# A new order for all engines' tasks in a forgetting-attention and gated-convolution kernel

## The chip, the core and the metric

The kernel runs on one core of a Trainium2 chip. A core has five engines that run side by side, each on its own instruction stream: PE (matrix multiply), DVE (vector), ACT (scalar functions), POOL (a slower general engine) and SP, which here does nothing but start DMAs. Each engine takes its instructions strictly in the order in which they were written. The metric is the device time of one execution in microseconds (us).

## The reference

Attention with a forgetting gate over 8 batches of 8 heads, 576 positions and 64 channels, and behind it a feed-forward layer with a convolution over the positions and a gate. Cut to what is computed:

```python
# _attn_ref(q, k, v, f)
scores = scale * np.matmul(q, k.transpose(0, 1, 3, 2))
log_f = np.log(np.clip(f, 0.0001, 1.0))
cum = np.cumsum(log_f, axis=-1)
decay = cum[:, :, :, None] - cum[:, :, None, :]
scores = np.where(causal, -1000000000.0, scores + decay)
attn = np.exp(scores - max); attn = attn / (sum + 1e-09)
return np.matmul(attn, v)
# _moe_ref(x, w_in, conv_w, w_out), x of shape (8, 576, 512)
h = np.maximum(x @ w_in, 0.0)                       # 512 -> 1024
conv_out += conv_w[k][None, None, :] * hp[:, k:k + S, :]   # three taps
gate = 1.0 / (1.0 + np.exp(-conv_out))
return (h * gate @ w_out)                           # 1024 -> 512
```

All inputs and the output are float32.

## The kernel before

The work is cut into tasks. A function `add(name, engines, after, fn, take, give, behind)` declares each: which engine may run it, what has to be done before it, and which buffers it takes and gives back. A table, `ORDER`, lists all the tasks in one row. `Plan.play` walks this row and calls each task's function at once, so the row is the program: every engine's instruction stream is the row with the other engines' tasks left out. Where a task may run on several engines, the row names one behind an `@`. Nothing sorts the tasks afterwards. Buffers are handed out first come, first served as the row is walked, so a task placed behind another may also get that one's buffer and must then wait for its reader.

The names. `hb` is half a batch, four heads, 0 to 15; `i` a pair of heads, two to an `hb`; `b` a batch; `ff` a block of 128 of the 1024 hidden channels.

- Loads on SP: `ld` (q and k of the first two `hb` as they are), `q` (q or k of a later `hb`, by a transposing DMA), `v`, `wi` and `wo` (the two weight matrices in four parts each).
- Decay: `dca` (DVE), `dcl` (ACT, a logarithm), `dcs` and `dck` (DVE) make the running sums; `ki` writes them to an image in DRAM, and `rw` or `fi` (three DMAs per `hb`, two for `rw`) fetch the rows of an `hb` from that image into its q and k tile, so that one matmul gives scores and decay. Of `hb` 0 the decay comes from extra matmuls instead, so it does not need `ki`.
- Setup: `tp` (PE) transposes the plainly loaded q and k, `cl` (DVE or ACT) copies them out or prepares the rows; `cw` (PE) and `cwt` (DVE) lay out the convolution's weights; `wic`, `woc` cast the weights to 16 bits and `va` casts v.
- Attention: `sd`, `so`, `st` (PE) make the diagonal, off-diagonal and last-64 scores; `ed`, `eo`, `et` (ACT) the exponentials; `md`, `mt` (POOL) mask where PE did not; `pv` (PE) multiplies with v in two parts; `n` and `m` (DVE) divide; `t` and `tx` turn the result for the next layer.
- Feed-forward: `f` (PE, first matmul), `r` (ACT, relu), `c` and `d` (DVE, the convolution), `a` (ACT, gate), `g` (DVE, product), `o` (PE, second matmul), `e` (ACT or DVE, out of PSUM), `s` (store).

PE writes into four PSUM tiles (`ps`) that all its tasks share. Five tiles `ht` hold `r`'s results until `g`, four tiles `u` hold `c`'s until `a`, four tiles `ob` stage weights and outputs, and four q and k tiles form a ring over `hb`. SP's and ACT's DMAs draw on eight semaphores in turn.

The lines to know in the profile are 159 (`ld`), 166 (`tp`), 172 and 174 (`cl` on ACT and DVE), 180 (`q`), 186 (`cl` of later rows), 204 and 205 (`rw`), 211 (`v`), 219 and 221 (`va`), 281 (`ki`), 296 (`cw`), 314, 317, 319 and 322 (scores), 355 and 372 (exponentials), 391 and 396 (`pv`), 407 (`m`), 416 and 419 (`t`, `tx`), 431 (`f`), 448 and 450 (`c`, `d`), 476 (`o`), 492 (the last `e`), 518 (`wi`, `wo`), 526 (`wic`, `woc`). The heart of `play`:

```python
for x in order:
    name, _, engine = x.partition("@")
    t = self.tasks[name]
    assert all(a in done for a in t["after"] + t["behind"]), name
    for r in t["take"]:
        self.slot[name, r] = free[r].pop(0)
    ...
    for r, taker in t["give"]:
        free[r].append(self.slot[taker, r])
```

## Time and profile before

| what | value |
|---|---|
| time, three runs | 245.07, 245.49 and 247.19 us, median 245.49 |
| profiled execution | span 244.7 us from its first to its last instruction; no other time of it is kept |
| busy in the span | PE 228.6 us (93%), ACT 206.8 (85%), DVE 205.5 (84%), POOL 51.9 (21%) |
| DMA | 49.68 MB, mean 203 GB/s; SP's queue carries 48.81 MB |

The profile is one execution. The median of the runs lies 0.8 us above its span. A line number stands for a function, so a group of instructions of one line is one kind of task; the number behind x is a count. In the table by windows each stretch has the busy time of every engine, the share of the full TensorE clock that was granted, and the mean load of the DMA engines. "PE ps L391 <- DVE va L219" in the table of waits reads: PE, about to write a `ps` tile at line 391, sat idle until DVE had written `va` at line 219. The chain of waits follows the last instruction back to what released it, step by step.

### The profile page before, as it was taken

To read this page: it belongs to the slowest core of one execution; us is meant where nothing else is said; L and a number is where in the kernel's file an instruction comes from. 1 tells how busy PE (TensorE), PEld (TensorE's weight loads), DVE (VectorE), ACT (ScalarE), POOL (GpSimd) and SP (SyncE) were. 2 spreads that over 40 slices of the span, in tenths; PEclk is the share of its full clock that TensorE was granted. 3 is DMA by queue.
4 is the path that set the end of the run, shared out by engine and by line. 5 is a ranking of instruction groups with operands and counts; after the bars stand their busy time and mean duration, and the time that the engine had idled before them with its cause. 6 is when DMAs were issued, how large, how long until landed. Compare 5 with 4: busy or idle time off the path is not lost.

```text
span 244.7 us, 6393 instructions
## 1 busy us (share of the span) xinstructions
PE 228.6 (93%) x2627; PEld 146.1 (60%) x2627; DVE 205.5 (84%) x324; ACT 206.8 (85%) x278; POOL 51.9 (21%) x77
## 2 busy tenths in 40 slices
...
GB/s 189 334 169 250 278 184 189 223 198 306 196 216 196 169 182 220 238 268 251 224 212 274 194 198 269 270 102 196 265 198 227 195 209 4 106 173 77 171 85 216
DMA packets 120424, 49.68 MB, mean 203 GB/s; under 512 B 109879, under 2 KB 110647, under 8 KB 120395
## 3 DMA queue, kind: packets, MB, share of 16 engines
q1 hardware_dynamic: 120073, 48.81, 89.9%
q10 hardware_dynamic: 322, 0.47, 0.6%
...
HBM read 21.11 MB, written 10.17 MB: 128 GB/s over the span
## 4 chain that ended last, share of the span: by engine, by line
PE 81%; DMA 5%; DVE 5%; ACT 5%; issue 1%; SPq 1%; ACTq 0%; DVEq 0%
PE ps L476 26%; PE ps L431 23%; PE ps L314 15%; PE ps L391 7%; DMA qk<-image 3%; PE ps L322 3%; PE ps L396 3%; DMA u<-in_f_dram 2%; PE ps L416 2%; ACT qk L172 2%; DVE u L450 2%; DVE u L448 1%; ACT ht L442 1%; ACT pp L372 1%; PE ps L317 1%
## 5 line engine op out<-in xcount | busy, mean ns | idle before, releaser
L431 PE MATMUL ps<-xt,w_in_f 128*128 128x512 f16 (+1 forms) x512 | 71.0, 288 | 0.4 <-DVE xt L419 0.4
L372 ACT ACTIVATE pp<-ps 128x1024 f16<-128x1024 f32 x64 | 64.8, 1032 | 3.7 <-PE ps L314 2.3
L476 PE MATMUL ps<-w_out_f,hg 128*128 128x512 f16 x288 | 66.8, 379 | 0.0
L314 PE MATMUL ps<-qk 128*128 128x128 bf16 (+2 forms) x576 | 63.9, 241 | 2.1 <-DMA qk<-image 0.9
L448 DVE SCALAR_TENSOR_TENSOR u<-ht,cwt 128x576 f32<-128x576 f16 x64 | 52.4, 832 | 4.4 <-ACT ht L442 4.2
L450 DVE SCALAR_TENSOR_TENSOR u<-ht,cwt,u 128x576 f32<-128x576 f16 x64 | 53.9, 856 | 0.5
L453 ACT ACTIVATE hg<-u,cw 128x576 f16<-128x576 f32 x64 | 48.7, 782 | 6.1 <-DVE u L450 6.0
L431 PEld LDWEIGHTS <-w_in_f 128*128 128x128 f16 x512 | 34.7, 99 | 29.4 <-issue 1.3
L314 PEld LDWEIGHTS <-qk 128*128 128x128 bf16 x576 | 39.4, 98 | 19.2 <-issue 2.5
L442 ACT ACTIVATE ht<-ps 128x576 f16<-128x576 f32 x64 | 41.0, 664 | 6.4 <-PE ps L431 2.8
L476 PEld LDWEIGHTS <-hg 128*128 128x128 f16 x288 | 26.9, 98 | 28.9
L460 DVE SCALAR_TENSOR_TENSOR hg<-hg,ht 128x576 f16<-128x576 f16 x51 | 38.6, 767 | 0.6 <-ACT hg L453 0.5
L358 POOL TENSOR_SCALAR_AFFINE_SELECT pp<-pd 128x1024 f16<-128x1024 f32 x16 | 19.7, 1244 | 53.6 <-ACT pd L355 53.6
L391 PE MATMUL ps<-va,pp 128*128 128x65 f16 x640 | 25.3, 194 | 1.7 <-DVE va L219 1.7
L391 PEld LDWEIGHTS <-pp 128*128 128x128 f16 x640 | 23.0, 98 | 4.2 <-DVE va L219 1.9
L407 DVE TENSOR_TENSOR xm<-ps,rc 128x896 f16<-128x896 f32 (+1 forms) x32 | 23.9, 751 | 0.5
L355 ACT ACTIVATE pp<-ps 128x1024 f16<-128x1024 f32 x16 | 16.6, 1038 | 5.2 <-PE ps L314 4.0
L219 POOL CAST va<-vf 128x1024 f16<-128x1024 f32 x8 | 10.0, 1247 | 34.3 <-PE ps L314 18.8
L355 ACT ACTIVATE pd<-ps 128x1024 f32<-128x1024 f32 x16 | 16.2, 1023 | 1.2 <-PE ps L314 0.5
L405 DVE RECIPROCAL rc<-ps 128x14 f32<-128x14 f32 (+1 forms) x32 | 6.6, 207 | 10.2 <-PE ps L396 4.9
L322 PE MATMUL ps<-mask,ident 128*128 128x512 bf16 (+1 forms) x40 | 14.4, 364 | 0.4 <-ACT pp L372 0.3
L481 ACT COPY ob<-ps 128x1024 f32<-128x1024 f32 (+1 forms) x14 | 12.9, 918 | 0.3 <-issue 0.2
...
## 6 DMA issues: line engine op xcount, KB each, us to landing
...
```

The lines of the kernel that those rows point to most:

```text
L314: nc.tensor.matmul(o, tk[:, h * S + k0:h * S + k0 + 128], tq[:, h * S + q0:h * S + q0 + n], start=first, stop=last and not by_matmul(hb, h))
L355: nc.scalar.activation(o, ps_of(f"sd{i}").rearrange("p (s c) -> p s c", s=2), AF.Exp, scale=SCALE)
L372: nc.scalar.activation(pair(i)[:, s, 512:1536], ps_of(f"so{i}.{s}"), AF.Exp, scale=SCALE)
L391: nc.tensor.matmul(ps[:, c:c + D + 1], block(hb, h, m, n), va[:, h, m, 0:D + 1], start=(m == 0), stop=(m == n))
L407: nc.vector.tensor_tensor(xm[:, CUT * D * u:CUT * D * u + nj * k * D].rearrange("p (j x d) -> p j x d", x=k, d=D), got[:, :, :, 0:D], r.un ...
L431: nc.tensor.matmul(ps[:, t0:t1], w_in_f16[:, cc, 128 * ff:128 * (ff + 1)], xt[:, cc // 2, x:x + t1 - t0], start=(cc == 0), stop=(cc == NCC ...
L442: nc.scalar.activation(ht_of(b, ff)[:, 2:2 + S], ps_of(f"f{b}.{ff}")[:, 0:S], AF.Relu, scale=1.0 if (b, ff) in LATE else 0.5)
L448: nc.vector.scalar_tensor_tensor(u, ht[:, 1:1 + S], cwt[:, ff, 0:1], ht[:, 2:2 + S], op0=ALU.mult, op1=ALU.add)
L450: nc.vector.scalar_tensor_tensor(u, ht[:, 3:3 + S], cwt[:, ff, 1:2], u, op0=ALU.mult, op1=ALU.add)
L453: nc.scalar.activation(hg_of(b, ff), u_t[slot[f"c{b}.{ff}", "u"]], AF.Sigmoid if (b, ff) in LATE else AF.Tanh, scale=cw[:, ff, 1:2])
L460: nc.vector.scalar_tensor_tensor(hv, hv, 1.0, ht_of(b, ff)[:, 2:2 + S], op0=ALU.add, op1=ALU.mult)
L476: nc.tensor.matmul(ps[:, 512 * j:512 * (j + 1)], w, w_out_f16[:, ff, :], start=(ff == 0), stop=(ff == NFF - 1))
```

## The change

Only the table `ORDER` is different; it now also runs over 52 lines more, so every later line of the new file has a number that is higher by 52 (159 becomes 211, and 211 becomes 263). The set of tasks is the same. 38 tasks change their engine:

- from DVE or ACT to POOL: `va1.1`, `va2.0`, `va3.0`, `va4.0`, `va7.0`, `va7.1`, `va8.0`, `va8.1`, `va9.0`, `va10.1`, `va11.1`, `va12.1`, `va14.0`, `va15.0`; from POOL to DVE or ACT: `va0.0`, `va0.1`, `va1.0`, `va9.1`, `wic0`
- from ACT to DVE: `cl0.0.0`, `va3.1`, `va5.1`, `va15.1`, `tx10`, `e1.1`, `e1.2`, `e2.0`, `e3.2`, `e7.4`; from DVE to ACT: `cl1.0.1`, `tx0`, `tx6`, `tx7`, `tx8`, `e4.0`, `e7.3`
- DMAs from SP to ACT's queue: `ki`, `rw1`, `rw6`, `s7.2`, `s7.0`; from ACT's to SP's: `rw4`, `rw5`

```diff
 ORDER = """
-dca cw ld0 ld1 ld0.0.0 tp0.0.0 dcl ld0.1.0 ld0.0.1 tp0.0.1 tp0.1.0 v0.0 ld0.1.1 ld1.0.1 ld1.0.0 dcs dck ...
+ld0 dca ld0.0.0 ld1 ld0.0.1 ld1.0.0 tp0.0.0 tp0.0.1 cl0.0.0@DVE ld1.0.1 dcl ld0.1.0 ld0.1.1 tp1.0.0 cl0.0.1@ACT v0.0
+tp1.0.1 dcs cl1.0.1@ACT v0.1 tp0.1.0 tp0.1.1 cl0.1.0@ACT v0.3 v0.4 dck q2.0 sd0 cl0.1.1@DVE tp1.1.0 v0.2 cl1.0.0@ACT
...
```

On PE the program no longer begins with `cw`: the first tasks are `tp0.0.0 tp0.0.1 tp1.0.0 tp1.0.1 tp0.1.0 tp0.1.1 sd0`, and `cw` follows seven tasks of scores and transposes later, behind `so0.1`. Up to the first `f0.0`, PE runs the same set of tasks as before, in another sequence; the same is true from `f0.0` to `sd9`.

SP near its start, from the end of the first v loads to the rows of `hb` 2 (`qk_86` and `qk_87` are the q and k tiles of `hb` 1 and 2, `vf_90` is v of batch 1, `ob` holds a part of `w_in`). Before:

```order
L281 DMA image<-kc 64x576 x3
L180 DMA_TRANSPOSE qk_87<-in_k_dram 128x2304
L180 DMA_TRANSPOSE qk_87<-in_q_dram 128x2304
L518 DMA ob_125<-in_moe_w_in_dram 128x2x512
L204 DMA qk_86<-image 1x2304
L205 DMA qk_86<-image 2x2304
L518 DMA ob_126<-in_moe_w_in_dram 128x2x512
L518 DMA ob_127<-in_moe_w_in_dram 128x2x512
L518 DMA ob_128<-in_moe_w_in_dram 128x2x512
L204 DMA qk_87<-image 1x2304
L205 DMA qk_87<-image 2x2304
```

Now, at the same place:

```order
L263 DMA vf_89<-in_v_dram 128x8x64 x3
L263 DMA vf_89<-in_v_dram 64x8x64
L232 DMA_TRANSPOSE qk_87<-in_q_dram 128x2304
L263 DMA vf_89<-in_v_dram 128x8x64
L232 DMA_TRANSPOSE qk_87<-in_k_dram 128x2304
L570 DMA ob_125<-in_moe_w_in_dram 128x2x512
L263 DMA vf_90<-in_v_dram 128x8x64
L570 DMA ob_126<-in_moe_w_in_dram 128x2x512
L256 DMA qk_87<-image 1x2304
L257 DMA qk_87<-image 2x2304
L570 DMA ob_127<-in_moe_w_in_dram 128x2x512
```

`ki` and the rows of `hb` 1 have left SP's queue, the rows of `hb` 2 stand behind two parts of `w_in` instead of four, and the transposing loads no longer stand behind `ki`.

ACT in the same stretch, from its first copy of q and k to its second exponential and a little on (`image<-kc` is `ki`, `pp` are exponentials, `pt` the last-64 ones). Before:

```order
L172 ACTIVATE qk_85<-ps_130,lim 128x1152
L172 ACTIVATE qk_85<-ps_131,lim 128x1152
L172 ACTIVATE qk_85<-ps_132,lim 128x1152
L355 ACTIVATE pp_95<-ps_131 128x2x512
L372 ACTIVATE pp_95<-ps_132 128x1024
L372 ACTIVATE pp_95<-ps_131 128x1024
L172 ACTIVATE qk_86<-ps_129,lim 128x1152
L355 ACTIVATE pp_96<-ps_132 128x2x512
```

Now:

```order
L407 ACTIVATE pp_95<-ps_132 128x2x512
L224 ACTIVATE qk_86<-ps_130,lim 128x1152
L333 DMA image<-kc 64x576 x3
L424 ACTIVATE pp_95<-ps_132 128x1024
L407 ACTIVATE pp_96<-ps_131 128x2x512
L256 DMA qk_86<-image 1x2304
L257 DMA qk_86<-image 2x2304
L386 ACTIVATE pt_101<-ps_129 128x256
L271 CAST va_92<-vf_89 128x4x4x64
L424 ACTIVATE pp_96<-ps_132 128x1024
```

ACT now starts `ki` and the rows of `hb` 1 itself, between its exponentials, and behind them stand `et0`, a cast of v and the rest of `hb` 0's exponentials.

POOL from its first cast on (`va_93` and `va_94` are v of `hb` 2 and 3). Before:

```order
L219 CAST va_91<-vf_89 128x4x4x64
L221 CAST va_91<-vf_89 64x4x64
L526 CAST w_in_f_69<-ob_125 128x2x512
L219 CAST va_92<-vf_89 128x4x4x64
L526 CAST w_in_f_69<-ob_126 128x2x512
```

Now:

```order
L578 CAST w_in_f_69<-ob_125 128x2x512
L273 CAST va_92<-vf_89 64x4x64
L578 CAST w_in_f_69<-ob_126 128x2x512
L578 CAST w_in_f_69<-ob_128 128x2x512
L271 CAST va_93<-vf_90 128x4x4x64
L273 CAST va_93<-vf_90 64x4x64
L271 CAST va_94<-vf_90 128x4x4x64
```

The casts of `hb` 2 and 3 that DVE and ACT had are POOL's now, and one of `w_in`'s four parts has gone to DVE.

More of the change, by code (lines that the diff above doesn't have):

```diff
@@ new lines @@
+ld0 dca ld0.0.0 ld1 ld0.0.1 ld1.0.0 tp0.0.0 tp0.0.1 cl0.0.0@DVE ld1.0.1 dcl ld0.1.0 ld0.1.1 tp1.0.0 cl0.0.1@ACT v0.0
+tp1.0.1 dcs cl1.0.1@ACT v0.1 tp0.1.0 tp0.1.1 cl0.1.0@ACT v0.3 v0.4 dck q2.0 sd0 cl0.1.1@DVE tp1.1.0 v0.2 cl1.0.0@ACT
+ed0 tp1.1.1 sd1 so0.1 cl1.1.1@ACT ki@ACT cl1.1.0@DVE cw cl2.0 q2.1 st0 eo0.1 wi1 ed1 rw1@ACT va0.0@DVE et0 so1.0
+va1.0@ACT eo1.0 so0.0 eo0.0 so1.1 v1.0 sd2 eo1.1 sd3 so3.0 va0.1@DVE cl2.1 ed2 pv0.0 wi2 cwt ed3 rw2@SP n0.0 wic1@POOL
+eo3.0 so2.1 m0.0 so2.0 wi0 pv0.1 n0.1 eo2.1 eo2.0 wic0@DVE so3.1 va1.1@POOL q3.1 m0.1 sd5 q3.0 eo3.1 ed5 pv1.0 st1 et1
@@ new lines @@
+t0 n1.0 pv1.1 m1.0 n1.1 tx0@ACT so5.1 m1.1 t1 tx1@DVE eo5.1 cl3.1 sd4 ed4 f0.0 r0.0 cl3.0 c0.0 so4.1 eo4.1 f0.1 d0.0
+r0.1 wi3 so4.0 q4.1 f0.2 c0.1 eo4.0 d0.1 r0.2 v1.3 wic2@POOL f0.3 rw3@SP h0 v1.2 a0.0 so5.0 r0.3 v1.1 wic3@POOL c0.2
+st2 g0.0 f0.4 v1.4 d0.2 c0.3 eo5.0 et2 sd6 va2.0@POOL sd7 r0.4 c0.4 cl4.1 so7.0 d0.3 so7.1 ed6 d0.4 ed7 eo7.0 so6.1
+pv2.0 f0.5 va2.1@POOL eo7.1 n2.0 q4.0 pv2.1 a0.4 v2.0 q5.0 wo3 m2.0 g0.4 cl4.0 rw4@SP so6.0 eo6.1 r0.5 va3.0@POOL f0.6
+eo6.0 n2.1 st3 c0.5 a0.3 v2.4 va3.1@DVE et3 pv3.0 r0.6 a0.1 pv3.1 d0.5 a0.2 n3.0 q5.1 m2.1 m3.0 wo1 n3.1 t2 g0.2 m3.1
@@ new lines @@
+g0.1 wo2 tx2@ACT f0.7 r0.7 sd9 a0.5 cl5.0 t3 so9.0 sd8 ed9 tx3@DVE wo0 c0.6 c0.7 eo9.0 so9.1 d0.6 f1.0 cl5.1 f1.1
+rw5@SP eo9.1 ed8 f1.2 g0.5 st4 r1.0 a0.6 v2.1 woc3@POOL d0.7 r1.1 f1.3 woc1@POOL g0.3 et4 g0.6 f1.4 a0.7 r1.2 g0.7
+so8.0 c1.1 r1.3 v2.2 woc2@POOL c1.3 v2.3 c1.0 eo8.0 so8.1 c1.2 d1.3 d1.2 f1.5 woc0@POOL d1.0 va4.0@POOL sd10 eo8.1
+r1.5 sd11 o0.0 h1 ed10 ed11 st5 a1.2 q6.1 va4.1@DVE a1.3 g1.2 so11.0 et5 eo11.0 o0.1 a1.0 d1.1 r1.4 va5.0@POOL g1.3
+pv4.0 c1.5 q6.0 e0.0@ACT n4.0 so10.1 f1.6 m4.0 so11.1 r1.6 o0.2 d1.5 cl6.1 a1.1 so10.0 eo10.1 cl6.0 c1.4 pv4.1 q7.1
@@ new lines @@
+rw6@ACT o0.3 d1.4 cl7.1 c1.6 q7.0 eo10.0 n4.1 eo11.1 pv5.0 sd13 zc m4.1 a1.5 e0.1@ACT va5.1@DVE v3.0 d1.6 g1.1 ed13
+cl7.0 v3.2 f1.7 so13.1 n5.0 v3.1 pv5.1 v3.4 r1.7 v3.3 eo13.1 m5.0 n5.1 m5.1 sd12 t4 a1.4 so12.1 rw7@SP ed12 tx4@DVE t5
+so13.0 so12.0 eo12.1 tx5@DVE st6 g1.4 eo13.0 et6 f2.0 f2.1 c1.7 eo12.0 r2.0 g1.0 a1.6 va6.0@POOL q8.0 d1.7 f2.2 sd15
+st7 g1.5 r2.1 sd14 c2.0 r2.2 ed15 et7 va7.0@POOL q9.1 f2.3 c2.2 va6.1@POOL d2.0 ed14 h2 va7.1@POOL a1.7 g1.6 so14.0
+eo14.0 r2.3 v4.0 pv6.0 f2.4 q9.0 g1.7 s0.1 d2.2 q8.1 r2.4 n6.0 a2.0 m6.0 f2.5 so15.0 c2.4 so15.1 a2.2 o1.0 eo15.1 fi9
@@ new lines @@
+so14.1 c2.1 g2.0 eo14.1 o1.1 d2.4 eo15.0 pv6.1 c2.3 d2.3 v4.3 r2.5 pv7.0 n6.1 m6.1 t6 a2.3 g2.3 e1.0@ACT f2.6 n7.0
+m7.0 c2.5 a2.4 g2.2 f2.7 d2.1 sd18 d2.5 v4.2 tx6@ACT r2.7 r2.6 fi8 c2.7 pv7.1 sd19 n7.1 ed18 ed19 o1.2 m7.1 d2.7
+so19.1 a2.1 a2.7 t7 st9 md19 c2.6 md18 tx7@ACT q11.0 g2.1 o1.3 eo19.1 g2.7 f3.0 et9 f3.1 e1.1@DVE q10.0 g2.4 a2.5
+q11.1 sd16 g2.5 r3.0 d2.6 q10.1 sd17 r3.1 c3.0 f3.2 ed16 so17.1 o1.4 d3.0 ed17 r3.2 e1.2@DVE so16.0 f3.3 so18.1 a2.6
+eo17.1 c3.2 c3.1 v4.1 g2.6 eo16.0 so18.0 r3.3 h3 eo18.0 md16 s0.0 so17.0 eo17.0 va8.0@POOL f3.4 fi11 fi10 d3.2 o2.0
@@ new lines @@
+so19.0 d3.1 r3.4 c3.4 a3.2 a3.1 st8 o2.1 g3.1 eo18.1 c3.3 eo19.0 et8 f3.5 d3.3 a3.0 md17 e2.0@DVE v4.4 g3.2 so16.1 mt9
+a3.3 s1.2 va9.0@POOL f3.6 pv9.0 eo16.1 sd22 mt8 r3.6 g3.3 r3.5 ed22 f3.7 d3.4 r3.7 sd20 pv8.0 c3.6 n9.0 ed20 so20.0
+m9.0 va8.1@POOL va9.1@DVE st10 et10 pv8.1 n8.0 m8.0 sd23 eo20.0 n8.1 md20 sd21 c3.7 pv9.1 v5.0 m8.1 ed23 so20.1 d3.7
+n9.1 c3.5 v5.3 q12.0 o2.2 m9.1 v5.2 a3.4 md22 t8 d3.6 eo20.1 g3.0 ed21 a3.7 a3.6 md21 tx8@ACT d3.5 t9 so21.0 tx9@DVE
+g3.6 o2.3 eo21.0 f4.0 q12.1 q13.0 g3.4 mt10 g3.7 a3.5 f4.1 v5.1 e2.1@ACT r4.1 f4.2 q13.1 f4.3 r4.2 va10.0@POOL r4.0
```

24 lines of the change are left out of this document (23 added, 1 removed).

## The prediction

> **What bounds the kernel now.** I read the span first, then the busy time of each engine in stretches cut where PE's work changes, then PE's waits, and last the timelines at the places that these name. The columns of the stretches: length, then busy us (and instructions) of PE, PE's weight loads, DVE, ACT and POOL, then granted clock, DMA share and GB/s.
>
> ```profile
> span 244.7 us, 6393 instructions
> ...
> 0.00:7.15 7.15, 0.00 (x0) 0.03 (x1) 3.24 (x19) 1.28 (x1) 5.37 (x31) 1.00 0.76 201
> 7.15:12.22 5.07, 4.98 (x45) 4.75 (x46) 4.03 (x11) 4.53 (x5) 0.00 (x0) 1.00 1.11 347
> 12.22:38.32 26.10, 24.12 (x357) 18.94 (x357) 11.62 (x19) 19.16 (x20) 6.52 (x7) 1.00 1.06 212
> 38.32:60.12 21.80, 19.01 (x248) 12.52 (x247) 20.44 (x30) 18.75 (x27) 2.88 (x3) 0.92 1.07 238
> 60.12:228.58 168.46, 168.45 (x1929) 104.56 (x1926) 157.57 (x236) 156.77 (x217) 37.17 (x37) 1.00 0.92 198
> 228.58:240.70 12.12, 12.09 (x57) 5.29 (x54) 8.16 (x13) 6.00 (x9) 0.00 (x0) 1.00 0.38 135
> 240.70:244.73 4.03, 0.00 (x0) 0.00 (x0) 0.42 (x1) 0.37 (x1) 0.00 (x0) 1.00 0.59 179
> ```
>
> PE is the bound, and it is saturated: of the 168.46 us from 60.12 on it works 168.45. An order that takes nothing away can't gain there. What PE loses is 12.22 us before the first score task `sd0` (of which 5 us are setup work), 26.10 − 24.12 = 1.98 us up to 38.32, 21.80 − 19.01 = 2.79 us up to 60.12, and 4.03 us behind its last matmul. Its waits between 12.22 and 60.12, and the one at the start, are these (total us, times, longest):
>
> ```profile
> PE ps L296 <- DMA pd<-in_moe_conv_w_dram: 7.2, 1, 7.2
> ...
> PE ps L391 <- DVE va L219: 1.7, 1, 1.7
> PE ps L314 <- DMA qk<-image: 0.9, 1, 0.9
> PE ps L314 <- ACT pp L355: 0.8, 2, 0.5
> PE ps L314 <- DVE xm L407: 0.5, 1, 0.5
> ...
> 50.40:52.00 1.60, 1.60 (x28) 1.36 (x25) 1.22 (x4) 1.60 (x4) 0.00 (x0) 0.52 1.26 285
> 52.00:54.00 2.00, 2.00 (x11) 0.92 (x9) 2.00 (x4) 2.00 (x4) 0.00 (x0) 0.53 1.12 224
> ```
>
> The last two rows are stretches again: right behind the 1.7-us wait PE runs at a granted clock of 0.52 and 0.53. So that stretch loses twice, 2.79 us of idling and, by its mean clock of 0.92, (1 − 0.92) × 21.8 = 1.7 us of slow work: 4.5 us.
>
> **The change, part by part.** The set of tasks stays, so each part is a shift of PE's idle time. I sum against the span of 244.7; the runs' median of 245.49 is 0.8 higher, which I carry over.
>
> *The start.* `cw` no longer stands first, so PE no longer waits for the last of the small loads; but now six transposes (54 instructions) stand ahead of `sd0` instead of four, and four of these need the loads of both halves.
>
> ```profile
> 7.15 0.98 PE L296 MATMUL ps<-one,pd 3*128 3x3 f32 x8 [7.15 <-DMA pd<-in_moe_conv_w_dram]
> 8.06 4.07 PE L166 MATMUL ps<-ident_b,hg 128*128 128x128 bf16 x36
> 12.22 0.58 PE L322 MATMUL ps<-mask,ident 128*128 128x512 bf16 x1
> ...
> 13.08 0.22 PE L314 MATMUL ps<-qk 128*128 128x128 bf16 x1
> ...
> GB/s 0 0 0 60 175 350 300 313 313 234 217 299 258 278 263 333 364 392 392 401 382 387 300 274 235 221 192 230 212 223 211 155 177 18 9 91 283 289 291 246
> ...
> 1.44 5.62 DMA u<-in_f_dram
> ```
>
> The GB/s row (slices of 0.5 us from zero) adds up to 2.6 MB at about 10.4 us. The q and k of batch 0, 2 × 8 × 576 × 64 × 4 bytes, and the gate's load of an eighth of that are just so much, and the new row issues them ahead of all v loads, so at the same rate the last of them is in by about 10.4. A load lands later than its bytes by this row: the gate's, issued beside three eighths of q and k, landed at 1.44 + 5.62 = 7.06, while the row has those three eighths at 5.0 and all four at 6.05, a lag of 1 to 2 us. So the last transposes may start at 11.4, and two of 9 instructions at 4.07/36 = 0.113 us each take 2.0 us: `sd0` at 13.4 instead of 12.22, **+1.2**. Ends: −0.8 (no lag, and one group of transposes behind the last load), +2.2 (a lag of 2). The 0.98 us of `cw` comes behind `sd0` and two groups of transposes come ahead of it, where they cost twice what they do later (the 13.08 row's kind of work is at full clock); I count these as even.
>
> *From `sd0` to 38.32.* The 0.9 us for `qk<-image` is `hb` 2's rows:
>
> ```profile
> 22.51 0.69 SPq L205 DMA_DIRECT2D qk<-image  x1
> 23.25 1.43 SPq L518 DMA_DIRECT2D ob<-in_moe_w_in_dram  x3
> ...
> 25.15 0.59 SPq L205 DMA_DIRECT2D qk<-image  x1
> ...
> 25.15 7.33 DMA qk<-image
> ...
> 25.68 0.38 PE L322 MATMUL ps<-mask,ident 128*128 128x512 bf16 x1
> ```
>
> The rows of `hb` 1 went out at 22.51 and PE's `sd2` used them at 25.68 to 25.9 without a wait, so they landed within 3.4 us; those of `hb` 2 went out behind all four parts of `w_in`, three of them just ahead, and took 7.33. Now `rw2` stands behind two parts and one v load of half a part's size: 0.75 MB less (1024 × 512 × 4 bytes in four parts), at the stretch's 212 GB/s 3.5 us, more than the 0.9 waited. Of the 1.98 us I take back **−1.7**, as the rest are single waits on ACT's exponentials, which stand closer to their scores now. Ends: 0 (DMA share is already 1.06) and −2.0. The transposing loads of `hb` 2 stand ahead of `rw2` before and now.
>
> *From 38.32 to 60.12.* The big wait:
>
> ```profile
> 45.66 1.54 DVE L448 SCALAR_TENSOR_TENSOR u<-ht,cwt 128x576 f32<-128x576 f16 x2 [0.61 <-ACT ht L442]
> ...
> 47.79 1.54 DVE L450 SCALAR_TENSOR_TENSOR u<-ht,cwt,u 128x576 f32<-128x576 f16 x2
> 49.25 0.68 DVE L219 CAST va<-vf 128x1024 f16<-128x1024 f32 x1
> ...
> 49.99 1.62 PE L391 MATMUL ps<-va,pp 128*128 128x65 f16 x32 [1.67 <-DVE va L219]
> ```
>
> The cast `va2.0` stands on DVE behind four convolution steps and a product, and `pv2.0` needs it. DVE is busy 20.44 of 21.80 us here, so whatever stands late on it is late for PE. The new row gives `va2.0` and `va3.0` to POOL, which works 2.88 us in this stretch, and puts several of the convolution's steps (`c0.6`, `c0.7`, `d0.6`) behind the division that PE waits for. With the 1.7-us wait go the idle time that precedes the half clock and, I think, the half clock itself. **−3.3** of 4.5: the whole of the 1.7, the slow work's 1.7 halved to 0.8, and 0.8 of the other waits, 2.79 − 1.67 = 1.1. Ends: 0 (a new wait of the same length) and −4.5. What is late next is DVE's division: the 0.5 us for `xm` above, which stays.
>
> *From 60.12 on.* POOL's added casts are off PE's path unless they slow DVE:
>
> ```profile
> 56.89 1.31 POOL L526 CAST w_out_f<-ob 128x1024 f16<-128x1024 f32 x1 [12.46 <-DMA ob<-in_moe_w_out_dram]
> ...
> 57.34 1.48 DVE L450 SCALAR_TENSOR_TENSOR u<-ht,cwt,u 128x576 f32<-128x576 f16 x1
> ...
> L450 DVE SCALAR_TENSOR_TENSOR u<-ht,cwt,u x64: 735/811/1651, 40.8 to 233.1; 128x576 f32<-128x576 f16 x64
> ```
>
> The row of L450 gives shortest, median and longest in ns. Next to a cast on POOL one DVE step took 1.48 us, the longest 1.65, against 0.81: a big cast can cost DVE up to 0.84 us. Six big and net four small casts come to POOL behind 60.12, 6 × 0.84 + 4 × 0.42 = 6.7 us at worst (a small one taken as half). DVE's other trades there:
>
> ```profile
> L419 DVE COPY xt<-ps 128x1152 f16<-128x1152 f16 x7 | 5.3, 754 | 1.4 <-PE ps L416 1.4
> L481 DVE COPY ob<-ps 128x1024 f32<-128x1024 f32 x3 | 3.7, 1219 | 2.0 <-ACT xt L419 1.9
> L219 DVE CAST va<-vf 128x1024 f16<-128x1024 f32 x3 | 3.0, 987 | 0.5 <-DMA out_dram<-ob 0.5
> L221 DVE CAST va<-vf 64x256 f16<-64x256 f32 x3 | 0.8, 257 | 0.0
> ```
>
> It gives off three big casts (3.0), two small (0.5), three `tx` (2.3) and `e4.0` (1.2), and takes `tx10` (0.75), two whole and two half evacuations (2.4 + 1.2) and three small casts (0.8): 7.0 off, 5.2 on, −1.8. So DVE's load here rises by 4.9 at most, and it has 168.46 − 157.57 = 10.9 us idle. PE didn't idle in this stretch although such steps occur in it; I take **+0.3**, ends 0 and +4.9. The Trainium skill, "SBUF — State Buffer", section "Who interferes with whom", says why: a DVE instruction with two inputs in SBUF needs the port that POOL reads through, and one of the two blocks. This rule speaks against the change, and the 1.48 us agrees.
>
> *The tail.* `e7.3` and `e7.4` swap DVE and ACT, and two stores go out on ACT. The last evacuations took 0.37 and 0.42 us of the 4.03; the rest is the store's way out. **0**, ends −0.2 and +0.6.
>
> Sum: 1.2 − 1.7 − 3.3 + 0.3 + 0 = −3.5; span 241.2, **242.0 us** as a run's time.
>
> **The rivals.** *B, the loads cap the lead:* DMA share is 1.06 and 1.07 up to 60.12, so rows, v and weights may come no earlier, and each wait removed returns as a wait for a load. Only the hole in the GB/s row at 16.5 to 18 us (18 and 9 GB/s) can be filled, 1.7 us of transfer: 245.5 − 1.7 = 243.8. Against it: PE's waits name DVE and ACT more than a DMA.
>
> *C, ACT's queue, slower:* `ki` and `rw1` now go out on ACT, in order. `ed0` began 2.28 us behind `sd0`:
>
> ```profile
> 14.50 1.02 ACT L355 ACTIVATE pp<-ps 128x1024 f16<-128x1024 f32 x1 [1.14 <-PE ps L319]
> ...
> 9.65 3.71 ACT L172 ACTIVATE qk<-ps,lim 128x1152 uint16<-128x1152 uint16 x3
> ...
> 13.48 1.82 SPq L281 DMA_DIRECT2D image<-kc  x3
> ```
>
> Now it would end at 13.4 + 2.3 + 1.0 = 16.7, the copy ahead of `ki` (3.71/3) at 17.9, and the last of the three issues starts at 17.9 + 2 × 0.6 = 19.1. If image transfers take 7.33 us each, as `rw2` did, `ki` lands at 26.4, `rw1`'s second half goes out at 26.9 and lands at 34.3, while `sd2` wants it at 25.9, and ACT's exponentials are held behind the issue: +8.4, **250.4 us**. It decides from landings of (25.9 − 19.1 − 0.5)/2 = 3.1 us. For it: v and q loads share the engines then. Against it: the same `hb` 1 rows landed within 3.4. The Trainium skill, "DMA: Bandwidth & Descriptors", section "Queues, rings and completion order", has each DMA engine take turns between the queues' rings; by that `rw1` would not stand behind all of SP's loads. No row here shows it.
>
> *D, DVE and POOL:* the load of +4.9 reaches PE in full, since relu tiles and `u` come free later: 245.5 − 3.8 + 4.9 = 246.6. Against it are the 10.9 idle us.
>
> That the change doesn't do what it says can be left out, since the row is played as it is written.
>
> **How the numbers follow.** Forecast 0.52 (its own range 239.5 to 243.2), B 0.22, C 0.15, D 0.11. A measurement of this kernel tells about 1% from no change: below 243.0 is faster, above 247.9 slower. Nearly all of the forecast's case is faster, 0.50, with a small part of B's 0.02; slower is C's 0.15 and 0.01 of D; the rest, 0.32, is the same. The range goes from 239.0, where nearly all of the first terms' far ends come together (−0.8 − 2.0 − 4.5 would be 238.2), to 247.5, which takes in B and D and leaves out C.
>
> **What would show it.** Start: the first L374 matmul (L322 before) between 12 and 15 us. Middle: no L443 wait (L391) for a cast on DVE, clock 0.97 or more between `f0.0` and `sd9`, and no wait for `qk<-image` over 1 us. Later: PE busy still equal to the stretch. I am wrong if PE waits for `image` rows at `sd2` (C), for `w_in`, v or q loads near 30 to 60 us (B), or if DVE's L500 and L502 rise to a mean above 0.9 us and PE idles behind 60 us (D).

## The result, and the profile after

The changed kernel took 256.3 us (median of four runs, 255.77 to 256.68) against 245.56 us before: a ratio of 1.043, with a 95% interval of 1.039 to 1.048. It is slower by 10.7 us, where 242.0 was forecast.

In its profiled execution the span is 255.0 us, and that execution's own time is 256.68, so 1.7 us lie around the span. First the stretches, cut at the events that the prediction speaks of: `sd0` at 13.40 us, `f0.0` at 37.60, `sd9` at 58.13, and the last matmul. Columns as in the prediction.

```profile
0.00:13.40 13.40, 6.27 (x54) 5.49 (x55) 7.57 (x24) 6.23 (x6) 5.37 (x31) 1.00 0.91 249
13.40:37.60 24.20, 23.21 (x345) 17.92 (x344) 11.63 (x24) 19.30 (x21) 2.41 (x3) 1.00 1.05 218
37.60:58.13 20.53, 17.57 (x255) 11.93 (x252) 19.54 (x28) 17.70 (x25) 4.50 (x5) 1.00 1.13 192
58.13:250.67 192.54, 182.52 (x1982) 109.88 (x1980) 182.72 (x250) 160.58 (x218) 54.61 (x48) 1.00 0.86 187
250.67:255.00 4.33, 0.00 (x1) 0.00 (x0) 0.42 (x1) 0.37 (x1) 0.00 (x0) 1.00 0.67 242
```

The new row is 2.0 us ahead at `sd9` (58.13 against 60.12) and then loses 12: from `sd9` to the last matmul it needs 192.54 us, where before needed 180.58:

```profile
60.12:240.70 180.58, 180.54 (x1984) 109.86 (x1980) 165.73 (x248) 162.76 (x226) 37.17 (x37) 1.00 0.88 194
```

PE, which was practically never idle there, now idles 10.0 us. The other 2.0 us are a longer busy time of PE (182.52 against 180.54), for which no run here shows a cause. PE waits behind `sd9` for ACT and DVE alone, most of all for these:

```profile
PE ps L483 <- ACT ht L494: 2.2, 2, 1.7
PE ps L366 <- ACT ht L494: 1.7, 2, 1.1
PE ps L366 <- DVE xt L471: 1.2, 1, 1.2
PE ps L443 <- DVE ob L533: 0.9, 1, 0.9
```

ACT in turn waits longer for DVE's second convolution step than before, 12.7 us instead of 6.0. The chain of work that ended last, by engine, was the first row before and is the second now:

```profile
PE 81%; DMA 5%; DVE 5%; ACT 5%; issue 1%; SPq 1%; ACTq 0%; DVEq 0%
```

```profile
PE 41%; DVE 35%; DMA 9%; ACT 8%; issue 3%; SPq 1%; ACTq 0%; DVEq 0%
```

What DVE does longer is on the page, first before, then after:

```profile
L448 DVE SCALAR_TENSOR_TENSOR u<-ht,cwt 128x576 f32<-128x576 f16 x64 | 52.4, 832 | 4.4 <-ACT ht L442 4.2
L450 DVE SCALAR_TENSOR_TENSOR u<-ht,cwt,u 128x576 f32<-128x576 f16 x64 | 53.9, 856 | 0.5
...
L460 DVE SCALAR_TENSOR_TENSOR hg<-hg,ht 128x576 f16<-128x576 f16 x51 | 38.6, 767 | 0.6 <-ACT hg L453 0.5
L358 POOL TENSOR_SCALAR_AFFINE_SELECT pp<-pd 128x1024 f16<-128x1024 f32 x16 | 19.7, 1244 | 53.6 <-ACT pd L355 53.6
```

```profile
PE 229.6 (90%) x2627; PEld 145.2 (57%) x2627; DVE 221.9 (87%) x324; ACT 204.2 (80%) x269; POOL 66.9 (26%) x86
...
L502 DVE SCALAR_TENSOR_TENSOR u<-ht,cwt,u 128x576 f32<-128x576 f16 x64 | 60.6, 960 | 0.5
L500 DVE SCALAR_TENSOR_TENSOR u<-ht,cwt 128x576 f32<-128x576 f16 x64 | 58.2, 925 | 2.0 <-ACT ht L494 1.9
...
L512 DVE SCALAR_TENSOR_TENSOR hg<-hg,ht 128x576 f16<-128x576 f16 x51 | 43.2, 859 | 1.8 <-ACT hg L505 1.7
L410 POOL TENSOR_SCALAR_AFFINE_SELECT pp<-pd 128x1024 f16<-128x1024 f32 x16 | 21.8, 1378 | 49.8 <-ACT pd L407 49.8
```

DVE does nearly the same steps as before, and its busy time rises from 205.5 to 221.9 us. The three groups of the convolution and the gate take 162.0 us instead of 144.9 (53.9 + 52.4 + 38.6). The masks on POOL, which the change does not touch, got slower as well, from a mean of 1.24 to 1.38 us. Where the two meet can be read off the timelines. POOL's first two masks before, and DVE beside them:

```profile
109.89 2.15 POOL L358 TENSOR_SCALAR_AFFINE_SELECT pp<-pd 128x1024 f16<-128x1024 f32 x2 [19.24 <-ACT pd L355]
...
109.65 1.09 DVE L407 TENSOR_TENSOR xm<-ps,rc 128x896 f16<-128x896 f32 x1
...
110.86 0.42 DVE L407 TENSOR_TENSOR xm<-ps,rc 128x256 f16<-128x256 f32 x1
111.56 0.76 DVE L419 COPY xt<-ps 128x1152 f16<-128x1152 f16 x1 [0.28 <-PE ps L416]
```

The first two masks after:

```profile
115.92 2.66 POOL L410 TENSOR_SCALAR_AFFINE_SELECT pp<-pd 128x1024 f16<-128x1024 f32 x2 [19.93 <-ACT pd L407]
...
115.98 1.65 DVE L502 SCALAR_TENSOR_TENSOR u<-ht,cwt,u 128x576 f32<-128x576 f16 x1
117.55 1.64 DVE L500 SCALAR_TENSOR_TENSOR u<-ht,cwt 128x576 f32<-128x576 f16 x1
```

Before, the masks stand beside DVE's divisions and copies, which read from PSUM and keep their usual length. After, they stand beside two convolution steps, and each of these takes twice its 0.81 us. Over the whole program, 4 of the 179 steps of these three groups took more than 1.3 us before, and 25 after. Of the sixteen big masks, 4 lay before beside DVE steps that were longer by over 0.2 us, and 14 after. Such longer steps are 7 before and 27 after, and every one of them overlaps a POOL instruction that reads SBUF. What they take beyond their usual length adds up to 4.0 us before and 21.3 after: 8.1 beside masks alone (1.6 before), 6.5 beside casts of v alone (0.8 before), 4.0 beside both (0.2) and 2.7 beside casts of weights (1.4).

### The profile page after: what moved, and what is told of

It is laid out like the page before. It is cut to its first block, busy times and chain, and to the rows that moved or that the text cites. A ratio compares the mean times of both kernels' runs of the same rounds, so it can differ in the third digit from the quotient of the medians.

```text
span 255.0 us, 6392 instructions
## 1 busy us (share of the span) xinstructions
PE 229.6 (90%) x2627; PEld 145.2 (57%) x2627; DVE 221.9 (87%) x324; ACT 204.2 (80%) x269; POOL 66.9 (26%) x86
## 4 chain that ended last, share of the span: by engine, by line
PE 41%; DVE 35%; DMA 9%; ACT 8%; issue 3%; SPq 1%; ACTq 0%; DVEq 0%
PE ps L528 16%; PE ps L483 10%; DVE u L500 10%; DVE u L502 9%; DVE hg L512 9%; PE ps L366 6%; PE ps L443 4%; ACT pp L424 3%; DMA hg<-in_k_dram 3%; DVE ob L533 2%; DVE xm L459 2%; DMA image<-kc 2%; ACT ht L494 2%; ACT hg L505 2%; PE ps L218 2%
## 5 line engine op out<-in xcount | busy, mean ns | idle before, releaser
L483 PE MATMUL ps<-xt,w_in_f 128*128 128x512 f16 (+1 forms) x512 | 69.7, 286 | 4.1 <-ACT ht L494 2.2
L424 ACT ACTIVATE pp<-ps 128x1024 f16<-128x1024 f32 x64 | 63.7, 1029 | 6.5 <-PE ps L366 2.4
L502 DVE SCALAR_TENSOR_TENSOR u<-ht,cwt,u 128x576 f32<-128x576 f16 x64 | 60.6, 960 | 0.5
L500 DVE SCALAR_TENSOR_TENSOR u<-ht,cwt 128x576 f32<-128x576 f16 x64 | 58.2, 925 | 2.0 <-ACT ht L494 1.9
L505 ACT ACTIVATE hg<-u,cw 128x576 f16<-128x576 f32 x64 | 48.6, 779 | 13.0 <-DVE u L502 12.7
L483 PEld LDWEIGHTS <-w_in_f 128*128 128x128 f16 x512 | 34.1, 98 | 32.9 <-issue 5.3
L512 DVE SCALAR_TENSOR_TENSOR hg<-hg,ht 128x576 f16<-128x576 f16 x51 | 43.2, 859 | 1.8 <-ACT hg L505 1.7
L410 POOL TENSOR_SCALAR_AFFINE_SELECT pp<-pd 128x1024 f16<-128x1024 f32 x16 | 21.8, 1378 | 49.8 <-ACT pd L407 49.8
L271 POOL CAST va<-vf 128x1024 f16<-128x1024 f32 x14 | 18.8, 1358 | 36.0 <-PE ps L366 17.5
L407 ACT ACTIVATE pp<-ps 128x1024 f16<-128x1024 f32 x16 | 16.2, 1040 | 0.7 <-PE ps L366 0.7
L238 DVE TENSOR_SCALAR qk<-qk,lim 128x2304 uint16<-128x2304 uint16 x12 | 11.8, 999 | 4.2 <-DMA qk<-in_k_dram 2.2
L218 PE MATMUL ps<-ident_b,hg 128*128 128x128 bf16 x72 | 7.7, 289 | 7.1 <-DMA hg<-in_q_dram 6.3
```

Source lines behind the costliest of these rows:

```text
L407: nc.scalar.activation(o, ps_of(f"sd{i}").rearrange("p (s c) -> p s c", s=2), AF.Exp, scale=SCALE)
L424: nc.scalar.activation(pair(i)[:, s, 512:1536], ps_of(f"so{i}.{s}"), AF.Exp, scale=SCALE)
L483: nc.tensor.matmul(ps[:, t0:t1], w_in_f16[:, cc, 128 * ff:128 * (ff + 1)], xt[:, cc // 2, x:x + t1 - t0], start=(cc == 0), stop=(cc == NCC ...
L500: nc.vector.scalar_tensor_tensor(u, ht[:, 1:1 + S], cwt[:, ff, 0:1], ht[:, 2:2 + S], op0=ALU.mult, op1=ALU.add)
L502: nc.vector.scalar_tensor_tensor(u, ht[:, 3:3 + S], cwt[:, ff, 1:2], u, op0=ALU.mult, op1=ALU.add)
L505: nc.scalar.activation(hg_of(b, ff), u_t[slot[f"c{b}.{ff}", "u"]], AF.Sigmoid if (b, ff) in LATE else AF.Tanh, scale=cw[:, ff, 1:2])
```

## The experiments

Three theories of the 12 us behind `sd9` were put against each other. Theory 1: the casts that came to POOL lock DVE. Theory 2: the new row moves POOL's work and DVE's against each other, so casts and masks alike now meet convolution steps; what counts is the place. Theory 3: the row orders DVE's and ACT's work badly, whatever POOL does.

All results in one table. The third column is the busy time of the three step groups on DVE (144.9 us in before's profile). Each ratio is taken against runs of the kernel before on the same chip, whose medians lay between 245.56 and 246.18 us.

| run | median us, ratio (95%) | steps, us |
|---|---|---|
| new row | 256.3, 1.043 (1.039 to 1.048) | 162.0 |
| e1 new row, casts back | 257.4, 1.048 (1.042 to 1.053) | 155.6 |
| e2 old row, casts' new engines | 252.4, 1.027 (1.023 to 1.032) | 153.3 |
| e3 new start, old rest | 248.4, 1.011 (1.005 to 1.017) | 146.9 |
| e4 new row, POOL only writes | 245.5, 1.000 (0.997 to 1.003) | 142.9 |
| e5 new row, masks only write | 250.2, 1.016 (1.008 to 1.023) | 149.4 |
| e6 new row, casts only write | 251.0, 1.019 (1.011 to 1.027) | 151.4 |
| e7 old row, masks 0.7 us late | 249.1, 1.012 (1.005 to 1.019) | 153.3 |
| e8 the same, masks only write | 245.7, 1.003 (1.000 to 1.007) | 145.9 |
| e9 old row, `va2.0` on POOL | 246.9, 1.002 (0.999 to 1.005) | 146.9 |
| e10 old row, five tasks put off | 250.7, 1.018 (1.013 to 1.023) | 144.4 |
| e11 e9 and e10 together | 251.7, 1.022 (1.018 to 1.026) | 144.5 |
| e12 old start, new rest | 255.5, 1.039 (1.033 to 1.044) | 159.2 |
| e13 e3 without its seam | 247.9, 1.010 (1.007 to 1.013) | 147.2 |
| e14 e1 with e5's masks | 256.2, 1.041 (1.035 to 1.046) | 144.4 |
| e15 old row, POOL only writes | 246.7, 1.003 (1.000 to 1.006) | 140.4 |

### Does POOL's reading make the loss?

The new row, with fills in place of POOL's casts of v and its masks (e4), then of the masks alone (e5) and of the casts alone (e6), and the same fills in the kernel before (e15):

```diff
-        copy = {"ACT": nc.scalar.copy, "POOL": nc.gpsimd.tensor_copy, "DVE": nc.vector.tensor_copy}[e]
+        copy = {"ACT": nc.scalar.copy, "POOL": lambda o, i: nc.gpsimd.memset(o, 0.01), "DVE": nc.vector.tensor_copy}[e]
...
-        nc.gpsimd.affine_select(pair(i)[:, :, 0:512].rearrange("p s (m j) -> p s m j", j=128),
...
+        nc.gpsimd.memset(pair(i)[:, :, 0:512], 0.01)
...
-        nc.gpsimd.affine_select(pt_t[slot[f"et{hb}", "pt"]], p3_t[slot[f"et{hb}", "p3"]],
...
+        nc.gpsimd.memset(pt_t[slot[f"et{hb}", "pt"]], 0.01)
```

> The new row, with POOL's casts of v and its masks each replaced by a fill of the same size: POOL works about as long at the same places but reads nothing. It leaves out the casting of v on POOL and the masking of the last eight half batches. Theories 1 and 2: no DVE step is longer than 0.9 us, DVE busy falls by 15 to 18 us to 204 to 207, time 243 to 246. Theory 3: DVE may be shorter, but the time stays at 252 to 256. If what locks is POOL's work and not its reading, nothing changes: 255 to 257.

> The new row, with the masks on POOL alone replaced by fills of the same size; the casts of v read as they do now. It leaves out the masking of the last eight half batches. Masks and casts both lock (theory 2): beside masks the convolution's steps got about 19 us longer, beside casts of v about 17 us, with much counted on both where a step meets two; so about half of the 10.8 us that the fills took off in all comes back, 249 to 252 us, DVE busy 211 to 215. If it is the masks alone: 245 to 247. If the casts alone: 255 to 257.

> The new row, with the casts of v that stand on POOL replaced by fills of the same size, and the masks as they are. It leaves out the cast of v for these 24 casts. Theory 2: 249 to 253 us, DVE busy 211 to 216. Masks alone: 255 to 257. Casts alone: 245 to 247.

> Control: the kernel before with the same fills in place of POOL's casts of v and masks. It leaves out these casts and the masking of the last eight half batches. Theory 2: before has little to lose by the lock, since its DVE steps beside POOL's reads get 6 us longer in all and its PE is busy anyway: 244 to 245.5, DVE busy 199 to 203. If the fills make any kernel much faster, and with it the new row's 10.8 us no sign of the lock: 236 to 241.

With all fills the kernel as a whole is as fast as before: 245.5 us. The page of e4, busy times and the second convolution step:

```profile
PE 227.7 (94%) x2627; PEld 145.5 (60%) x2627; DVE 202.7 (83%) x324; ACT 203.4 (84%) x269; POOL 46.3 (19%) x86
...
L445 DVE SCALAR_TENSOR_TENSOR u<-ht,cwt,u 128x576 f32<-128x576 f16 x64 | 51.7, 822 | 0.5
```

DVE's busy time falls by 19 us, although POOL still works 46 us at its places in the row. Five steps stay long, all beside the casts of weights, which still read; none is long beside a fill alone. The masks alone give back 6.1 us, the casts alone 5.3, together 11.4 where both at once gave 10.8.

The fills also free POOL from waiting for its inputs, which is a gain of its own ahead of `sd9`: in e4 `sd9` comes at 56.29 us instead of 58.13. Behind `sd9`, to the last matmul, e4's row is:

```profile
56.29:239.00 182.71, 180.28 (x1982) 109.63 (x1980) 164.44 (x250) 159.75 (x218) 35.44 (x48) 1.00 0.92 197
```

So of the 12.0 us that the new row loses behind `sd9`, 9.8 go with POOL's reads (192.54 to 182.71), and 2.1 stay. With the masks as fills (e5) the same stretch takes 185.63 us, with the casts as fills (e6) 187.08: 6.9 and 5.5 less. Each of these stretches is from one profiled execution. In this stretch of the new row PE waits for POOL nowhere, and its weight loads do once, for 1.2 us, so an earlier POOL has little to give there by itself. Theory 3 therefore falls as the main cause, and the loss is shared about evenly between casts, 14 of them new on POOL, and masks, of which none is new. On the kernel before the same fills give nothing (e15, 1.003), although its DVE steps fall from 144.9 to 140.4 us: before's PE is busy all the time behind `sd9` and has no use for a faster DVE.

### Is it the place?

The kernel before, with each big mask held back by reading one number of its input and then filling a tile that is no longer used (e7), and the same with a fill in place of the mask (e8):

```diff
+        nc.gpsimd.tensor_copy(hfx[:, 0:1], pd_t[slot[f"ed{i}", "pd"]][:, 1, 511:512])
+        nc.gpsimd.memset(zero[:, 0:640], 0.0)
         nc.gpsimd.affine_select(pair(i)[:, :, 0:512].rearrange("p s (m j) -> p s m j", j=128),
```

> The kernel before, unchanged but for this: each of POOL's sixteen big masks is held back by about 0.7 us, by reading one number of its input and then a fill of a tile that is no longer used. Nothing else moves. Theory 2, before is fast because its masks happen to stand beside DVE's divisions and copies, which read one operand from SBUF or none: shifted, they meet convolution steps, the time that these take beyond 0.81 us beside the big masks rises from 3.4 us to 8 us or more, DVE busy by 4 us or more, time 248 to 252. If the place in time doesn't matter: 245 to 246.5, DVE busy up by under 1 us.

> Control for the one before: the same delay, and behind it a fill in place of the mask, so POOL comes as late but reads nothing. It leaves out the masking of the last eight half batches on the diagonal. Theory 2: 244.5 to 246.5, DVE busy 203 to 206. If the late mask itself holds up PE: as slow as the one before, 248 to 252.

The pages of both, busy times, e7 above e8:

```profile
PE 227.9 (92%) x2627; PEld 145.0 (59%) x2627; DVE 213.0 (86%) x324; ACT 207.1 (84%) x278; POOL 63.5 (26%) x109
```

```profile
PE 228.5 (94%) x2627; PEld 145.8 (60%) x2627; DVE 206.3 (85%) x324; ACT 207.3 (85%) x278; POOL 60.1 (25%) x109
```

The delay alone costs 3.5 us and lengthens DVE's work by 7.5 us; nothing has changed but the place in time of sixteen POOL instructions and the 32 short ones that hold them back, which e8 has too. Most of the steps' growth is the gate's product (38.6 to 45.1 us), where the convolution had been expected. With a fill in place of the mask, as late and behind the same read of one number, the time is that of before. The held-back masks were delayed by more than planned (the read and the fill took 0.3 and 0.6 us), which does not matter for the contrast of the two.

### Casts or row?

The new row with the 21 casts of v that had changed engine back on theirs (e1; the lists of the change hold 43 tasks, not 38, and these are 21 of them), the old row with those engines changed (e2), and e1 with the masks as fills (e14). One of the 21 in each:

```diff
-... va4.0@POOL ...
+... va4.0@ACT ...
```

> The new row, but each cast of v stands on the engine that it had before (14 of them leave POOL again, some of them for DVE and ACT). Theory 1, POOL's added casts lock DVE's port: DVE's convolution steps fall back from 0.93 and 0.96 us to about 0.84 and 0.86, PE idles little behind 60 us, time 243 to 246. Theory 2, the row puts POOL's casts and masks alike beside the convolution's steps: the masks stay there, DVE keeps over half of its extra 16 us, time 250 to 254. Theory 3, the row orders DVE's and ACT's work badly whatever POOL does: time 253 to 258.

> The row of before with nothing changed but the engines of the casts of v, which are those of the new row. Theory 1: 250 us or more, DVE busy up by 8 us or more. Theory 2: DVE gets longer by at most 0.84 us for each of eight big casts less what leaves DVE, which its idle 10 us takes in part: 246 to 249. Theory 3: no change, 245 to 246.

> The new row with both: the casts of v on their engines of before, and the masks as fills of the same size. It leaves out the masking of the last eight half batches. Theory 2: what was left of the loss with the casts back was the masks beside convolution steps, so 245 to 249. If the casts, back on DVE and ACT at places that were chosen for POOL, hold up PE by themselves: 251 to 257.

On the old row the engines alone cost 6.4 us, the time that theory 1 had named (DVE busy rose by 5.7 us, to 211.2, where it had named 8). But only 2.1 us of that are lost behind `sd9`, where the stretch takes 182.70 us; `sd9` itself comes at 63.99, 3.9 us late, behind waits of PE for DVE and ACT. So this run does not show that the casts' reads cost 6.4 us. On the new row, taking them back gains nothing: 257.4, which is where theory 3 had put it, and theories 1 and 2 both missed. Theory 2 had put this down to the masks; e14 contradicts that, since with the masks as fills the steps are down to 144.4 us and the time is still 256.2, with 192.20 us behind `sd9`. So this part of theory 2 fell. In e14 PE is held up by other waits, the same that e1 has (a timeline of PE, rows with a wait; e14, then e1):

```profile
67.78 1.14 PE L426 MATMUL ps<-xt,w_in_f 128*128 128x512 f16 x8 [1.33 <-ACT ht L437]
...
75.12 0.38 PE L322 MATMUL ps<-mask,ident 128*128 128x512 bf16 x1 [2.48 <-ACT pp L367]
```

```profile
66.19 1.14 PE L431 MATMUL ps<-xt,w_in_f 128*128 128x512 f16 x8 [1.39 <-ACT ht L442]
...
73.24 0.38 PE L322 MATMUL ps<-mask,ident 128*128 128x512 bf16 x1 [2.18 <-ACT pp L372]
```

PE waits on ACT there, and in e14 also 1.7 us for casts of v on DVE. The casts stand on ACT and DVE at places in the row that suited POOL, and each holds up what is queued behind it. That this is the whole of e14's 10 us is argued from the waits, not shown: no run moved these casts to other places. So e1 and e14 do not tell theory 1 from theory 2, and with the casts back the row is slow whether the masks read or not; e4 to e6 and the pair of e7 and e8 do tell them apart.

### Which part of the row, and is the lead at 58 us a gain?

The new row up to `sd9` with the old rest (e3), the old row up to `sd9` with the new rest (e12), and e3 with two of ACT's tasks moved behind three exponentials (e13; the diff is that of e3's row, without the engines' names):

```diff
-... sd9 wo0 cl5.0 c0.6 d0.6 v2.3 c0.7 a0.5 woc3 woc1 a0.6 t3 so9.1 st4 ed9 et4 eo9.1 sd8 ...
+... sd9 wo0 cl5.0 c0.6 d0.6 v2.3 c0.7 woc3 woc1 t3 so9.1 st4 ed9 et4 eo9.1 a0.5 a0.6 sd8 ...
```

> The new row up to sd9 (about 58 us), and behind it the remaining tasks in the sequence and on the engines of before. All theories have the gain of the first 60 us as real, 2.0 to 2.3 us at sd9: theories 1 and 2 give 243 to 244 us, since 14 casts behind 60 us and the masks stand as before. If the loss behind 60 us comes out of the first part (buffers or loads handed over later), 248 to 256.

> The row of before up to sd9, and the remaining tasks in the sequence and on the engines of the new row. Theory 2, the new row's later part puts POOL's reads beside the convolution's steps: 253 to 258 us, DVE's convolution steps at 0.90 us or more. If the loss needs the new row's first part (its 2 us of lead or its DVE debt): 246 to 250.

> As the splice of the new start on the old rest, but with a0.5 and a0.6 on ACT behind ed9, et4 and eo9.1, where the new row has them too; in the splice they stood ahead, and PE idled 3.2 us behind sd9. If that idling came of the seam alone, the new start's 2 us of lead stay: 243 to 244.5, faster than both kernels. If DVE's steps that were put off behind sd9 (3.3 us) have to be paid in any case: PE idles 2 us or more elsewhere between 60 and 109 us, 245.5 to 248.

The rest alone carries 9.3 of the 10.7 us (e12), so most of the loss needs nothing of the first part. The first part, which led at `sd9`, ends 2.4 us behind when the old rest follows it (e3), where theories 1 and 2 had expected it to be faster than before. The stretches behind `sd9`, e12's and then e3's:

```profile
59.82:249.12 189.30, 181.95 (x1985) 109.67 (x1980) 177.82 (x248) 160.00 (x217) 51.99 (x46) 1.00 0.85 183
```

```profile
57.44:241.07 183.63, 180.42 (x1982) 109.86 (x1980) 168.69 (x251) 163.54 (x227) 37.20 (x37) 1.00 0.87 198
```

Behind the new start the new rest takes 192.54 us instead of 189.30, and the old rest 183.63 instead of 180.58. In both pairs the new start makes what follows 3.1 to 3.2 us longer, more than the 1.7 and 2.7 us by which it leads at `sd9` (58.13 against 59.82, 57.44 against 60.12). Each figure is from one profiled execution. PE's waits behind `sd9` in e3, then in e13:

```profile
PE ps L322 <- ACT pp L355: 3.2, 1, 3.2
```

```profile
63.56 0.65 PE L431 MATMUL ps<-xt,w_in_f 128*128 128x512 f16 x4 [2.19 <-DVE xt L419]
```

Moving the two tasks took e3's wait away, and another of 2.2 us stands 0.7 us later, on DVE. So the lead was not kept in either splice. (In the new row `a0.5` stands directly behind `sd9` and `a0.6` ahead of `et4`, not behind all three exponentials as the expectation has it, so e13's order of ACT is one of its own.)

The middle of the new row was also tried by itself on the old one: `va2.0` on POOL (e9), the five tasks `cl5.0`, `c0.6`, `d0.6`, `c0.7`, `a0.6` behind `sd9` (e10), and both (e11).

```diff
-... va2.0@DVE ... cl5.0 ... c0.6 ... d0.6 ... c0.7 ... a0.6 ... m3.1 sd9 t3 ...
+... va2.0@POOL ... m3.1 sd9 cl5.0 c0.6 d0.6 c0.7 a0.6 t3 ...
```

> The kernel before with one task on another engine: the cast va2.0, for which PE waited 1.67 us, goes from DVE to POOL. The prediction's third term: the wait goes and with it some of the half clock, 243 to 244.5 us. The other reading, that DVE sets the pace up to 60 us and beyond: DVE is freed of 0.68 us, so 244.5 to 245.5, with a new wait of PE on DVE or ACT before 65 us. If the POOL cast meets a convolution step and locks it: 245.5 to 246.5.

> The kernel before with five tasks moved behind sd9, as the new row has them: cl5.0, c0.6, d0.6, c0.7 on DVE and a0.6 on ACT. They are 3.3 us of DVE's work. If this is a gain, as the prediction's third term had it: sd9 earlier by 1 us or more and 243.5 to 244.5. If it is a debt: sd9 earlier, but PE idles as much more between 60 and 109 us, 245.5 to 247.5.

> The two before together, the middle part of the new row alone. The prediction's third term: -3.3, 242 to 243. The debt's reading: 245 to 247, sd9 2 to 3 us earlier and PE idle by 2 us or more between 60 and 109 us.

PE's waits in e9 at the place of the 1.67-us wait, and the cast on POOL:

```profile
48.00 1.15 PE L391 MATMUL ps<-va,pp 128*128 128x65 f16 x32 [0.51 <-POOL va L219]
52.20 0.27 PE L322 MATMUL ps<-mask,ident 128*128 128x256 bf16 x1 [1.38 <-ACT pp L355]
```

```profile
46.41 1.54 POOL L219 CAST va<-vf 128x1024 f16<-128x1024 f32 x1 [13.60 <-DMA vf<-in_v_dram]
```

The wait for the cast shrinks from 1.67 to 0.51 us, and a new one of 1.38 us on ACT follows; `sd9` comes 0.5 us earlier and the time is not shorter. All three runs took longer than any of their expectations had it. The five tasks put off cost 4.5 us; behind `sd9` PE is idle in one wait, and works 1.5 us longer besides (182.08 us):

```profile
65.05 0.38 PE L322 MATMUL ps<-mask,ident 128*128 128x512 bf16 x1 [4.17 <-ACT pp L355]
```

Here `a0.6` stands on ACT ahead of the exponentials of `hb` 4, and it waits for DVE's late step. The new row has `ed9`, `eo9` and `ed8` ahead of it, so e10 and e11 price the debt in the old row's sequence of ACT and not the new row's. For the new row the price is the 3.2 us against e12; which of its tasks make it stays open. None of the kernels tried beats the kernel before.

## Why the prediction was wrong

Against the terms of its sum, by the stretches above:

- **Start, +1.2:** `sd0` came at 13.40 us, the time forecast, but by two misses that cancel. PE's last wait for a load ended at 10.55 us and not at 11.4, and three groups of transposes stood behind it, not two; that is luck.

```profile
10.55 3.06 PE L218 MATMUL ps<-ident_b,hg 128*128 128x128 bf16 x27 [0.36 <-DMA hg<-in_k_dram]
```

  Two readings in this term were a little off and move nothing: the GB/s row has the four eighths at 6.2 us, not 6.05, and the early transposes cost 1.5 times the later ones (1.02 against 0.67 us for nine), not twice.
- **`sd0` to `f0.0`, −1.7:** 24.20 us instead of 37.30 − 12.22 = 25.08, so −0.9, inside the bounds (the prediction cut at 38.32, the second group of `f0.0`'s matmuls, 1.02 us later). The rows did come early enough for `hb` 2, whose wait of 0.86 us is gone. (What `rw2` no longer stands behind is 0.79 MB and 3.7 us by the prediction's own figures, not 0.75 and 3.5.) What was not in the sum is a small form of rival C: ACT, with `ki` and `rw1` in its own stream, stood still:

```profile
23.99 0.38 ACT L386 ACTIVATE pt<-ps 128x256 f16<-128x256 f32 x1 [2.48 <-DMA image<-kc]
```

  PE's wait for these rows, those of `hb` 1 at `sd2`, was 0.4 us, so C in its priced form did not happen.
- **`f0.0` to `sd9`, −3.3:** 20.53 instead of 60.12 − 37.30 = 22.82, so −2.3. The size is inside the bounds, the way to it is not the one forecast: of the 3.3, 2.5 were to be waits that go and 0.8 slow work. The half clock is gone (1.00), and PE's busy time fell by 2.1 us (19.67 to 17.57), but its idle time by only 0.2 (3.15 to 2.96), since the 1.67 us came back as two waits. Before's row of this stretch, then the two waits:

```profile
37.30:60.12 22.82, 19.67 (x256) 12.85 (x252) 21.26 (x31) 19.47 (x28) 2.88 (x3) 0.93 1.06 228
```

```profile
48.48 1.15 PE L443 MATMUL ps<-va,pp 128*128 128x65 f16 x32 [1.21 <-POOL va L271]
...
52.95 0.60 PE L366 MATMUL ps<-qk 128*128 128x64 bf16 x4 [1.66 <-DVE xm L459]
```

- **Behind `sd9`, +0.3, the step that failed:** +12.0. The prediction saw the mechanism and priced one meeting rightly: up to 0.84 us for a DVE step beside a POOL read, and the steps after show 1.65 against 0.81. It counted only the casts that were new on POOL and let the masks cost what they had cost before, as if the place of POOL's work on DVE's time line were a given. By e5 half of the loss is the masks'. Nor is 0.84 us the most that a step can lose: three of the 25 steps over 1.3 us lost 0.9 to 1.3 us, each beside two or more POOL reads in a row. The longest, of the first convolution step, took 2.11 us (shortest, median and longest in ns below). The end of +4.9 was therefore no bound.

```profile
L500 DVE SCALAR_TENSOR_TENSOR u<-ht,cwt x64: 731/810/2106, 40.0 to 242.7; 128x576 f32<-128x576 f16 x64
```

- **The lead as a gain:** the sum carries what the first 58 us gain over to the end. The runs do not: the new start with the old rest ends 2.4 us behind (e3), and with POOL's casts of v and masks only writing the new row is no faster than before (e4, 1.000). So even without most of the loss to POOL the forecast would not have come true.
- **DVE's 10.9 idle us as cover:** they covered only a part. In e2 and e7 the steps grew by 8.4 us, and behind `sd9` 2.1 and 3.6 us were lost. In the new row they grew by 17.1 us, more than all of that idle time, and DVE took 35% of the chain: its waits for ACT before the convolution fell (4.2 to 1.9 us), and the waits of ACT for DVE's second step rose.

```profile
L453 ACT ACTIVATE hg<-u,cw 128x576 f16<-128x576 f32 x64 | 48.7, 782 | 6.1 <-DVE u L450 6.0
```

```profile
L505 ACT ACTIVATE hg<-u,cw 128x576 f16<-128x576 f32 x64 | 48.6, 779 | 13.0 <-DVE u L502 12.7
```

  The first row is before, the second after. Rival D, given 0.11 and 246.6 us, was the one that came true, at more than twice its price; both of its signs are there, means of 0.925 and 0.960 us and an idle PE. Rival B did not come: between `sd0` and the last matmul PE waited 0.4 us for a DMA in all.
- **Tail, 0:** 4.33 against 4.03 us, +0.3, inside its bounds.

The terms as measured, 1.2 − 0.9 − 2.3 + 12.0 + 0.3, are the 10.3 us between the two spans. The 0.8 us carried from span to time was no property of the kernel: in the runs that keep both, an execution's time is 1.7 to 1.9 us above its span. By that, an estimate, the profiled execution of before took about 246.5 us and was merely one of the longer ones.

The Trainium skill's rule of "SBUF — State Buffer", section "Who interferes with whom", which the prediction weighed against this change, held in more of its parts than were used: POOL work that only writes does not block such a DVE step (in e4 none is long beside a fill alone), and a DVE instruction with at most one input in SBUF, outside the modes in which it uses two ports, does not contend with POOL (the divisions and the copy at 109.65 to 111.56 us keep their usual 1.09, 0.42 and 0.75 us).
